# A routing-attention kernel: the first q and k loaded by tokens and turned by TensorE

## The chip, the core and the metric

The kernel runs on one core of a Trainium2 chip. Its engines are TensorE (matmuls, results into PSUM), VectorE, ScalarE and GpSimd (elementwise work), and SyncE, which issues DMAs; ScalarE issues some too. Each engine takes its instructions in order, and they meet by semaphores. The metric is the device time of one execution in microseconds (us): the median of several runs. Beside it stands one profiled execution, whose trace the views below are made from.

## The reference

An attention block with a mask by clusters, followed by a feed-forward block. Cut to what matters:

```python
# q, k, v: (4, 8, 768, 64); centroids: (8, 16, 64)
q_assign = argmax(einsum('bhsd,hcd->bhsc', normed(q), normed(centroids)))
k_assign = argmax(einsum('bhsd,hcd->bhsc', normed(k), normed(centroids)))
mask = q_assign[:, :, :, None] == k_assign[:, :, None, :]
scores = where(mask, q @ k.T / sqrt(64), -1e9)
attn = softmax(scores)
x = (attn @ v), heads side by side: (3072, 512)
h = x @ w_in                       # (512, 2048)
g = h * erf(softplus(h))
out = g @ w_out                    # (2048, 512)
```

All of it is float32. The centroid with the greatest similarity decides a token's cluster; a query sees only the keys of its own cluster.

## The kernel before

**Staging.** Heads are worked in pairs: 4 batches of 4 pairs make 16, and a pair's two heads lie in partitions 0 to 63 and 64 to 127. For each pair the kernel needs q and k with the head dimension in the partitions and the 768 tokens in the columns (tiles `qT` and `kT`, 128 x 768, float32). Period by period (`period(p, i)`, lines 1432 to 1536) it makes scores on TensorE, exponentials on ScalarE, sums on GpSimd and the product with v on TensorE, while parts of the coming pairs and of the weights are prepared on the side. Behind the attention stands the feed-forward block, which is nearly all TensorE.

**How q and k come in.** `load` (lines 225 to 246) fetches q in four DMAs: for each head `e` and each half `g` of its 64 dimensions, 32 partitions take the tokens of a block, and within them 24 runs of 32 float32 numbers:

```python
queues[e if nm == "q" else e * g].dma_start(
    out=t[e * D + g * Q : e * D + (g + 1) * Q],
    in_=src[b, h0 + e, :, g * Q : (g + 1) * Q].rearrange("(n t) d -> t n d", t=Q),
)
```

A block of 32 tokens by 32 dimensions then lies the wrong way round, and VectorE's transpose, which turns each 32 x 32 block, makes `qT` of `in_q` in one instruction; the same for k. For pair 0, `queues` is SyncE and ScalarE (q half and half, k with one DMA on ScalarE and three on SyncE); line 260 then sets both to SyncE, and pair 1 is loaded into the tile `x_more` by eight DMAs.

**The prologue** (lines 253 to 279, 349 to 389, 1543 to 1600) is written out by hand, and `InOrder` (lines 126 to 139) keeps each engine's instructions in program order. It runs like this:

- The centroids come in by a DMA of their own and are normed by VectorE and ScalarE (the tile `pr`, of which `cn` is a part). TensorE transposes `cn` with the identity (`te.transpose`, line 1546, into `pct`, a part of the bank `turned`), and two ScalarE copies put it into `ccT`. This is called the pct transpose below.
- `warm(n, bank, rhs)` (lines 1539 to 1541) issues n matmuls whose results nobody reads: 13 of 256 columns on the still empty tile `pick` at the start, 4 of 384 columns on zeros behind the pct transpose, 9 more before the masks, and 2 between the steps of the maxima.
- `qT` and `kT` of pair 0 are made (lines 1550 and 1556). ScalarE casts them to bfloat16 (`vectors`: `qv`, `kv`).
- `similarities(0)` (lines 404 to 415) multiplies `ccT` with both halves of `qT` and of `kT`: four 32-column groups, each in two passes, into `turned`. `choose(0)` (lines 417 to 441) is a chain on VectorE: transpose to `sims`, maximum, comparison (`hot`), transpose to `hotT`.
- In between, eight VectorE copies (lines 1562 to 1569) fill `pick`, a 0/1 matrix made of `first`, which GpSimd builds; `products(0)` makes the first q-by-k products into a PSUM tile `sc`.
- `masks(0, ...)` (lines 447 to 469) multiply `pick` with `hotT` and write `qm` and `km`. `maxima_step(0, i)` (lines 473 to 504), six of them, multiply `qv` by `kv` and `qm` by `km` on TensorE and take the maximum over the keys by VectorE (`nmx`); they use the PSUM tiles `wide` and `also` in turn.
- Then the first period starts.

`ps_s` is a pool of two PSUM tiles of 128 x 2 x 512 that `sc` and `also` come from by turns; `wide` is a third such tile of its own. `stage` holds one `in_q` and one `in_k`, so the loads of pair 2 (`load_qk(2)`) wait until pair 0's have been read.

Of the kernel before, what the change touches and what calls it, by code (L numbers as in the profile page):

```python
# [9 lines left out]
F32 = mybir.dt.float32  # L10
# [9 lines left out]
P = 128  # L20
B, H, S, D = 4, 8, 768, 64
C = 16
NJ = S // P
Q = 32
NB = S // Q
HW = S // 2
QW = HW // 2
TW = QW + 1
HJ = NJ // 2
# [113 lines left out]
def kernel(  # L143
# [13 lines left out]
    te, ve, ae, ge = (  # L157
        InOrder(tc, e, in_order) for e in (nc.tensor, nc.vector, nc.scalar, nc.gpsimd)
    )
# [8 lines left out]
    turned = [ps.tile([P, 512], F32, name=f"turned{i}") for i in range(2)]  # L168
# [12 lines left out]
    def passing(name, bufs, **kw):  # L181
        return attention.enter_context(tc.tile_pool(name=name, bufs=bufs, **kw))

    ps_s = passing("ps_s", 2, space=PSUM)
    wide = passing("ps_w", 1, space=PSUM).tile([P, 2, 512], F32, name="wide")

    const = passing("fixed", 1)
    stage = passing("stage", 1)
# [4 lines left out]
    ident = const.tile([P, P], F32, name="ident")  # L193
    identb = const.tile([P, P], BF16, name="identb")
    first = const.tile([P, P], BF16, name="first")
    pick = const.tile([P, 2, P], BF16, name="pick")
# [15 lines left out]
    rows = [{nm: const.tile([P, S], F32, name=f"{nm}T{i}") for nm in "qk"} for i in range(2)]  # L212
# [5 lines left out]
    pairs = {}  # L218
    sy = InOrder(tc, nc.sync, in_order)
    queues = [sy, ae]  # L220

    def heads(p):
        return p // HP, 2 * (p % HP)

    def load(p, nm, src, pl):
        if p >= NPAIR:
            return
        b, h0 = heads(p)
        if nm == "v":
            t = pl.tile([P, NJ, 2, D], F32, name="in_v")  # L230
            for e in range(2):
                queues[0].dma_start(out=t[:, :, e], in_=src[b, h0 + e].rearrange("(j p) d -> p j d", p=P))
        else:

            if pl is None:
                t = x_more.rearrange("p a k t -> p (a k t)")[:, (nm == "k") * S : (1 + (nm == "k")) * S]
                t = t.rearrange("p (n t) -> p n t", t=Q)
            else:
                t = pl.tile([P, NB, Q], F32, name="in_" + nm)
            for e in range(2):  # L240
                for g in range(D // Q):
# [4 lines that stand above are left out]
        pairs.setdefault(p, {})[nm] = t  # L246
# [7 lines left out]
    cen = setup[:, 0:D]  # L254
    sy.dma_start(out=cen, in_=centroids.rearrange("h c d -> (h c) d"))

    load(0, "q", q, stage)
    tc.keep_in_program_order(nc.scalar.preload_act_table_set("natural_log_exp_and_others"))
    load(0, "k", k, stage)
    queues[1] = sy  # L260
    load_qk(1)

# [6 lines left out]
    for base, pattern, sign, op, fill in (  # L269
# [5 lines left out]
            out=first, in_=first, compare_op=op, fill=fill, base=base, pattern=pattern,  # L275
# [141 lines left out]
    def choose(p, spare=None, aside=False):  # L417

        if p >= NPAIR:
            return  # L420
        st = pairs[p]
        n = HW // C
        sims = routep.tile([P, HW], F32, name="sims")
        ve.transpose(out=sims, in_=st.pop("psim"))
        yield
        sim = sims.rearrange("p (g c) -> p g c", c=C)
        mx = (wide[:, 0] if spare is None else spare)[:, 512 - n :]
        ve.reduce_max(out=mx, in_=sim, axis=AX.X)
        yield
        hot = routep.tile([P, HW], BF16, name="hot")  # L430
        ve.tensor_tensor(
            out=hot.rearrange("p (g c) -> p g c", c=C), in0=sim,
            in1=mx.unsqueeze(2).to_broadcast([P, n, C]), op=ALU.is_equal,
        )
        yield
        if aside:
            st["aside"] = routep.tile([P, HW], BF16, name="aside")
            ve.transpose(out=st["aside"][D + Q :], in_=hot[D : D + Q])
            yield
        st["hotT"] = routep.tile([P, HW], BF16, name="hotT")  # L440
        ve.transpose(out=st["hotT"], in_=hot)
# [84 lines left out]
    def products(u):  # L526
        p, half, j = units[u]
        if u in sc_of:
            return
        st = pairs[p]  # L530
        sc = sc_of[u] = ps_s.tile([P, 2, 512], F32, name="sc", tag="s")
        for e in range(2):
            r = slice(e * D, (e + 1) * D)
            te.matmul(
                sc[:, e, 0:HW], lhsT=st["kT"][r, j * P : (j + 1) * P],
                rhs=st["qT"][r, half * HW : (half + 1) * HW], start=True, stop=False,
            )
# [874 lines left out]
    def run(work):  # L1412
        for _ in work:
            pass
# [124 lines left out]
    def warm(n, bank, rhs):  # L1539
        for _ in range(n):  # L1540
            te.matmul(bank[:, 0 : rhs.shape[-1]], lhsT=identb, rhs=rhs, start=True, stop=True)

    zeros = lowest[1].rearrange("p t n -> p (t n)")
    warm(13, turned[1], pick.rearrange("p h n -> p (h n)"))
    pct = turned[0][:, 0:P]
    te.transpose(out=pct, in_=cn.rearrange("p e d -> p (e d)"), identity=ident)
    warm(4, turned[1], zeros)
    st = pairs[0]
    st["qT"], st["kT"] = rows[0]["q"], rows[0]["k"]
    ve.transpose(out=st["qT"], in_=st.pop("q").rearrange("p n t -> p (n t)"))  # L1550
    for e in range(2):
        ae.copy(
            out=ccT[e * D : (e + 1) * D, :, e * C : (e + 1) * C],
            in_=pct[e * D : (e + 1) * D].rearrange("d (r e c) -> d r e c", e=2, c=C)[:, :, e],
        )
    ve.transpose(out=st["kT"], in_=st.pop("k").rearrange("p n t -> p (n t)"))
    st.update(lows[0])
    load_qk(2)
    similarities(0)
# [2 lines left out]
    for r in (0, D):  # L1562
        for half in range(2):
            for e in range(2):
                c = r + half * Q + e * C
                ve.tensor_copy(
                    out=pick[r : r + D, half, e * D : (e + 1) * D].rearrange("p (n c) -> p n c", n=2)[:, :, 1 : C + 1],
                    in_=first[r : r + D, c : c + C].unsqueeze(1).to_broadcast([D, 2, C]),
                )
    also = ps_s.tile([P, 2, 512], F32, name="sc", tag="s")  # L1570
    products(0)
    warm(9, turned[0], zeros)
    run(choose(0))
    copies = [
        masks(0, nm, half, bank)
# [144 lines left out]
```

## Time and profile before

| What | Value |
|---|---|
| Median of 3 runs | 950.66 us (950.62 to 950.67) |
| Profiled execution, its own time | 950.97 us |
| Its span, first to last instruction | 949.2 us |
| DMA in all | 136.15 MB, 143 GB/s on average |
| TensorE's granted clock, all 40 slices | 0.9 or more |

How to read the views: a row of the page's groups names line, engine, operation, output and inputs, how often, busy time, mean time of one in ns, and the idle time before. Nearly all operations here have the line 134, that of the helper `InOrder`, so rows are told apart by their tiles. PE is TensorE, PEld its weight loads, DVE VectorE, ACT ScalarE, POOL GpSimd, SP SyncE; a "q" behind the name is the engine's queue, where DMAs are issued. In a timeline row the first number is the start in us, the second the stretch that the row covers, and the bracket behind tells how long the engine was idle before and what ended that. Matmul ends are modelled.

### The profile page before, as it was taken

The page shows a single profiled execution, that of the slowest core. Times are in us where ns is not written, and L with a number is a line of the kernel's source. Part 1 is how long each engine was busy: PE and PEld are TensorE (multiplying, and loading weights), DVE is VectorE, ACT ScalarE, POOL GpSimd, SP SyncE. Part 2 cuts the span into 40 slices and gives each one's busy share as a digit, 9 for nine tenths or more (in the row PEclk, how much of TensorE's full clock was granted, in tenths as well). Part 3 has the DMA queues.
Part 4 walks back from the last instruction along what each step waited for, and adds up shares of the span by engine and source line. Part 5 has one row for each costly group of instructions (what it writes and reads, how often), then busy time and mean ns, then how long its engine had stood idle before and what let it go on. Part 6 is the DMA issues. An engine that isn't in the chain of part 4 may idle for free.

```text
span 949.2 us, 20906 instructions
## 1 busy us (share of the span) xinstructions
PE 941.6 (99%) x8167; PEld 695.6 (73%) x8167; DVE 752.9 (79%) x1310; ACT 554.8 (58%) x852; POOL 557.5 (59%) x381
## 2 busy tenths in 40 slices
PE   8999999999999999999999999999999999999998
PEld 3555555555555555588888888888888888888887
DVE  8888888888888887788879878456786974768977
ACT  3788888888887665557523542357825225675341
POOL 1688888888888888845779930576600028770000
PEclk9999999999999999999999999999999999999999
DMA  9444544647454314292895486556645435533443
GB/s 208 93 114 107 116 108 109 156 113 200 91 113 107 71 34 146 81 326 67 164 192 212 155 238 216 156 155 175 191 141 182 156 112 154 171 97 114 153 133 111
DMA packets 181730, 136.15 MB, mean 143 GB/s; under 512 B 131808, under 2 KB 141536, under 8 KB 181600
## 3 DMA queue, kind: packets, MB, share of 16 engines
q1 hardware_dynamic: 174416, 125.21, 45.9%
q0 software_dynamic: 4720, 9.18, 5.5%
q8 instruction: 65, 1.06, 0.5%
q10 hardware_dynamic: 2496, 0.43, 0.2%
q14 instruction: 33, 0.27, 0.1%
HBM read 95.72 MB, written 40.89 MB: 144 GB/s over the span
## 4 chain that ended last, share of the span: by engine, by line
PE 97%; DVE 1%; DMA 0%; ACT 0%; issue 0%; DVEq 0%
PE bank L134 45%; PE turned L134 30%; PE sc L134 17%; PE wide L134 6%; DVE nmx L134 1%; DMA pr<-in_centroids_dram 0%; DMA in_q<-in_q_dram 0%; DVE pr L134 0%; ACT pr L134 0%; DVE sims L134 0%; DVE qT L134 0%; ACT qm L134 0%; DVE turned L134 0%; DVE wide L134 0%; ACT km L134 0%
## 5 line engine op out<-in xcount | busy, mean ns | idle before, releaser
L134 POOL TENSOR_TENSOR more_out<-more_out,pr 128x768 f32<-128x768 f32 x128 | 222.4, 1738 | 17.5 <-ACT pr L134 9.7
L134 DVE TENSOR_REDUCE nmx<-wide 128x2 f32<-128x512 f32 (+2 forms) x189 | 180.7, 956 | 57.8 <-PE wide L134 56.8
L134 ACT ACTIVATE pr<-sc 128x768 f32<-128x768 f32 x192 | 148.6, 810 | 71.5 <-PE wide L134 63.9
L134 PE MATMUL turned<-pr,in_v 128*32 128x193 f32 x3072 | 144.9, 330 | 0.0
L134 PEld LDWEIGHTS turned<-pr,in_v 128*32 128x32 f32 x3072 | 91.5, 109 | 51.5 <-issue 25.5
L134 PE MATMUL sc<-qT,kT 64*128 64x384 f32 x528 | 98.7, 487 | 0.0
L134 POOL TENSOR_TENSOR more_out<-pr,pr 128x768 f32<-128x768 f32 x32 | 58.7, 1834 | 46.6 <-ACT pr L134 46.6
L134 POOL TENSOR_TENSOR u<-w_in 128x1 f32<-128x1 f32 x2 | 0.4, 189 | 138.6 <-DVE w_in L134 138.6
L134 PE MATMUL bank<-x_own,more_in 128*128 128x256 f32 x280 | 69.1, 379 | 0.0
L134 PE MATMUL bank<-g_more,more_in 128*128 128x256 f32 x288 | 66.5, 380 | 0.0
L134 PE MATMUL wide<-kv,qv 64*128 64x256 bf16 (+2 forms) x378 | 64.2, 328 | 1.3 <-DVE nmx L134 0.7
L134 DVE TENSOR_TENSOR g<-g 128x512 f32<-128x512 f32 x70 | 48.6, 695 | 19.3 <-PE bank L134 12.3
L134 PE MATMUL wide<-km,qm 64*128 64x256 bf16 (+3 forms) x378 | 62.6, 327 | 0.0
L134 PEld LDWEIGHTS sc<-qT,kT 64*128 64x128 f32 x528 | 48.0, 187 | 19.5 <-ACT inv L134 3.2
L134 PEld LDWEIGHTS bank<-g_more,more_in 128*128 128x128 f32 x288 | 54.6, 190 | 8.2 <-DVE g L134 0.8
L134 PEld LDWEIGHTS bank<-x_own,more_in 128*128 128x128 f32 x280 | 53.2, 190 | 7.2
L134 DVE TENSOR_TENSOR g<-g,bank 128x256 f32<-128x256 f32 (+1 forms) x85 | 41.9, 511 | 20.4 <-PE bank L134 12.7
L134 ACT ACT_TABLE_LOAD x36 | 46.2, 1283 | 18.4 <-DVE g L134 17.8
L134 PE MATMUL bank<-w_out,g 128*128 128x256 f32 x240 | 55.2, 379 | 0.0
L134 DVE TENSOR_TENSOR g<-a_s,g 128x512 f32<-128x512 f32 x56 | 51.8, 941 | 2.7 <-ACT a_s L134 2.7
L134 PEld LDWEIGHTS <-qv 64*128 64x128 bf16 x384 | 22.8, 93 | 41.4 <-issue 25.3
L134 ACT ACTIVATE x_own<-x_own 128x512 int32<-128x512 uint32 (+2 forms) x52 | 52.7, 1028 | 0.0
(253 smaller groups left out, 2148.3 us busy)
## 6 DMA issues: line engine op xcount, KB each, us to landing
more_in<-a_dram SPq DMA_DIRECT2D x98, 256.0 KB, 2.7
g_more<-b_dram SPq DMA_DIRECT2D x48, 512.0 KB, 3.6
x_own<-in_moe_w_in_dram SPq DMA_DIRECT2D x13, 512.0 KB, 3.6
in_v<-in_v_dram SPq DMA_DIRECT2D x32, 192.0 KB, 3.1
x_dram<-more_out SPq DMA_DIRECT2D x128, 48.0 KB, 2.5
a_dram<-w_in SPq DMA_DIRECT2D x12, 512.0 KB, 5.0
x_own<-x_dram SPq DMA_DIRECT2D x6, 1024.0 KB, 5.9
in_k<-in_k_dram SPq DMA_DIRECT2D x59, 96.0 KB, 2.7
```

The lines of the kernel that those rows point to most:

```text
L134: ins = getattr(self.engine, name)(*args, **kw)
```

## The change

Four things. First, pair 0's q and k are no longer fetched by `load`, but with the tokens in the partitions: two DMAs each, one a head, one on SyncE and one on ScalarE, 768 runs of 64 numbers each. Second, TensorE turns them: six transposes with the identity for q into `wide`, six for k into a tile of `ps_s`; ScalarE copies the one to `qT`, VectorE the other to `kT`. These stand ahead of the pct transpose. VectorE's two block transposes go. Third, the eight copies into `pick` move from VectorE to GpSimd. Fourth, of the matmuls of `warm` there are 5 instead of 13, 3 instead of 4 and 8 instead of 9. The loading of the activation table on ScalarE now stands behind both of its DMAs, as before behind its two q loads.

Behind the prologue the two kernels have the same instructions in the same order on each engine.

```diff
-    load(0, "q", q, stage)
+    by_token = {}
+    for nm, src in (("q", q), ("k", k)):
+        t = stage.tile([P, NB, Q], F32, name="in_" + nm).rearrange("p n t -> p (n t)")
+        by_token[nm] = t.rearrange("p (j e d) -> p j e d", j=NJ, e=2)
+        for e in range(2):
+            queues[e].dma_start(out=by_token[nm][:, :, e], in_=src[0, e].rearrange("(j p) d -> p j d", p=P))
     tc.keep_in_program_order(nc.scalar.preload_act_table_set("natural_log_exp_and_others"))
-    load(0, "k", k, stage)
     queues[1] = sy
     load_qk(1)
...
     zeros = lowest[1].rearrange("p t n -> p (t n)")
-    warm(13, turned[1], pick.rearrange("p h n -> p (h n)"))
+    warm(5, turned[1], pick.rearrange("p h n -> p (h n)"))
+    st = pairs[0] = {}
+    rooms = {"q": wide, "k": ps_s.tile([P, 2, 512], F32, name="sc", tag="s")}
+    for nm in "qk":
+        for j in range(NJ):
+            te.transpose(
+                out=rooms[nm][:, j // HJ, j % HJ * P : (j % HJ + 1) * P],
+                in_=by_token[nm][:, j].rearrange("p e d -> p (e d)"), identity=ident,
+            )
+        st[nm + "T"] = rows[0][nm]
+        copy = ae.copy if nm == "q" else ve.tensor_copy
+        copy(out=st[nm + "T"].rearrange("p (h t) -> p h t", h=2), in_=rooms[nm][:, :, 0:HW])
     pct = turned[0][:, 0:P]
     te.transpose(out=pct, in_=cn.rearrange("p e d -> p (e d)"), identity=ident)
-    warm(4, turned[1], zeros)
-    st = pairs[0]
-    st["qT"], st["kT"] = rows[0]["q"], rows[0]["k"]
-    ve.transpose(out=st["qT"], in_=st.pop("q").rearrange("p n t -> p (n t)"))
+    warm(3, turned[1], zeros)
     for e in range(2):
         ae.copy(
             out=ccT[e * D : (e + 1) * D, :, e * C : (e + 1) * C],
             in_=pct[e * D : (e + 1) * D].rearrange("d (r e c) -> d r e c", e=2, c=C)[:, :, e],
         )
-    ve.transpose(out=st["kT"], in_=st.pop("k").rearrange("p n t -> p (n t)"))
     st.update(lows[0])
...
                 c = r + half * Q + e * C
-                ve.tensor_copy(
+                ge.tensor_copy(
...
     products(0)
-    warm(9, turned[0], zeros)
+    warm(8, turned[0], zeros)
     run(choose(0))
```

## The prediction

> **What bounds the kernel now.** I read the page first: engine shares, then the chain that ended last.
>
> ```profile
> span 949.2 us, 20906 instructions
> ...
> PE 941.6 (99%) x8167; PEld 695.6 (73%) x8167; DVE 752.9 (79%) x1310; ACT 554.8 (58%) x852; POOL 557.5 (59%) x381
> ...
> PE 97%; DVE 1%; DMA 0%; ACT 0%; issue 0%; DVEq 0%
> ...
> L134 ACT ACTIVATE pr<-sc 128x768 f32<-128x768 f32 x192 | 148.6, 810 | 71.5 <-PE wide L134 63.9
> ```
>
> TensorE is the chain for 97% of the span, so whatever the changed prologue gains or loses moves the rest one for one: the order of the instructions behind the prologue is the same in both kernels, and their loads can only be issued earlier. The prologue is the stretch in which TensorE is not the bound. So I read its timeline, engine by engine (start, length, engine, operation, what ended the idle time before it): SyncE's queue, TensorE, VectorE, ScalarE, GpSimd.
>
> ```profile
> 1.26 0.98 SPq L134 DMA_DIRECT2D in_q<-in_q_dram  x2
> 2.29 2.10 SPq L134 DMA_DIRECT2D in_k<-in_k_dram  x3
> ```
>
> ```profile
> 2.41 2.96 PE L134 MATMUL turned<-pick,identb 128*128 128x256 bf16 x13 [2.41 <-DVE fixed L134]
> 5.54 0.45 PE L134 MATMUL turned<-ident,pr 128*128 128x128 f32 x1 [0.17 <-DVE pr L134]
> 5.78 1.49 PE L134 MATMUL turned<-lowest,identb 128*128 128x384 bf16 x4
> 7.19 0.82 PE L134 MATMUL turned<-qT,ccT 128*32 128x384 f32 x2
> 7.70 0.57 PE L134 MATMUL turned<-kT,ccT 128*32 128x384 f32 x2
> 7.83 0.50 PE L134 MATMUL turned<-qT,ccT 128*32 128x384 f32 x2
> 8.10 0.49 PE L134 MATMUL turned<-kT,ccT 128*32 128x384 f32 x2
> 8.52 0.92 PE L134 MATMUL sc<-qT,kT 64*128 64x384 f32 x4
> 9.37 1.64 PE L134 MATMUL turned<-lowest,identb 128*128 128x384 bf16 x9
> 11.07 0.32 PE L134 MATMUL wide<-hotT,pick 64*128 64x384 bf16 x1
> ```
>
> ```profile
> 4.97 0.42 DVE L134 TENSOR_SCALAR pr<-pr 128x64 f32<-128x64 f32 x2
> 5.30 0.97 DVE L134 STREAM_TRANSPOSE qT<-in_q 128x768 f32<-128x768 f32 x1
> 6.66 0.98 DVE L134 STREAM_TRANSPOSE kT<-in_k 128x768 f32<-128x768 f32 x1 [0.39 <-DMA in_k<-in_k_dram]
> 7.57 0.80 DVE L134 COPY pick<-first 64x32 bf16<-64x32 bf16 x8
> 8.64 0.58 DVE L134 STREAM_TRANSPOSE sims<-turned 128x384 f32<-128x384 f32 x1 [0.28 <-PE turned L134]
> 9.26 0.56 DVE L134 TENSOR_REDUCE wide<-sims 128x24 f32<-128x384 f32 x1
> 9.85 0.55 DVE L134 TENSOR_TENSOR hot<-sims,wide 128x384 bf16<-128x384 f32 x1
> 10.44 0.58 DVE L134 STREAM_TRANSPOSE hotT<-hot 128x384 bf16<-128x384 bf16 x1
> 11.43 0.56 DVE L134 TENSOR_SCALAR qm<-wide 128x384 bf16<-128x384 f32 x1 [0.41 <-PE turned L134]
> 11.90 0.97 DVE L134 STREAM_TRANSPOSE qT<-x_more 128x768 f32<-128x768 f32 x1
> 12.79 0.92 DVE L134 TENSOR_REDUCE nmx<-wide 128x2 f32<-128x768 f32 x1
> ```
>
> ```profile
> 6.02 0.42 ACT L134 COPY ccT<-turned 64x64 f32<-64x64 f32 x2 [1.92 <-PE turned L134]
> ```
>
> ```profile
> 2.87 0.77 POOL L134 MEMSET lowest<- 128x384 bf16 x2
> ```
>
> What to see: the last k load lands at 6.66 (VectorE was waiting for it), kT ends at 7.64, the k similarities follow at 7.70 and end at 8.59, then `sims` to `hotT` on VectorE until 11.02, the mask matmuls at 11.07, and VectorE's chain of maxima from 12.79. So one number decides: the end of the k similarities, 8.59 us. The eight pick copies lie behind kT, but VectorE still waits 0.28 us for TensorE after them: they cost nothing now.
>
> TensorE's own rate changes here too. In the row of 4 a 384-column matmul takes some 0.32 us from start to start, in the row of 9 (1.64 less 0.33 for the last, by 8) 0.16. The first q pair takes 0.64 to its second pass (7.19 to 7.83), the k pair's second pass only 0.40 (7.70 to 8.10): full rate comes at about 7.8, 5.4 us after the first matmul. The profile's granted clock reads 1.00 throughout and doesn't show it.
>
> **The loads.** Removed are eight loads of 96 KB (four of q, four of k) in runs of 32 numbers, 128 bytes; added are four of 192 KB in runs of 64, 256 bytes: half the packets, the same 786 kB. The centroids (33 kB) stay ahead. Rates, from the view of stretches (last columns: DMA share, GB/s), and a load's time to landing, from the view of DMA issues:
>
> ```profile
> 1.50:2.00 0.50, 0.00 (x0) 0.00 (x0) 0.26 (x6) 0.17 (x1) 0.43 (x7) 1.00 0.15 33
> 2.00:2.50 0.50, 0.09 (x1) 0.10 (x2) 0.41 (x7) 0.50 (x1) 0.43 (x2) 1.00 1.09 184
> 3.50:4.00 0.50, 0.50 (x4) 0.38 (x3) 0.13 (x1) 0.30 (x2) 0.14 (x1) 1.00 1.37 213
> 5.00:5.50 0.50, 0.36 (x2) 0.00 (x0) 0.50 (x3) 0.00 (x0) 0.00 (x0) 1.00 1.39 216
> 5.50:6.00 0.50, 0.46 (x2) 0.36 (x3) 0.50 (x1) 0.00 (x0) 0.00 (x0) 1.00 0.97 150
> 48.25:48.50 0.25, 0.25 (x4) 0.00 (x0) 0.25 (x1) 0.25 (x1) 0.25 (x1) 1.00 1.08 244
> ```
>
> ```profile
> in_q<-in_q_dram SPq DMA_DIRECT2D x1, 96.0 KB, 3.2
> ```
>
> The first row puts the first bytes near 1.95 us; the next three are the rate with 128-byte runs while loads are queued; the row at 48 us is a stretch in which only in_v moves, whose loads have the very form of the new ones. The last is q's last load (issued near 1.72): landed near 4.9. I take 244 GB/s. The bounds: 216 (longer runs bring nothing) and 314 (244 if packets overlapped on the engines as at 5 us, 1.39 over 1.08). From last byte to landing I take 0.4 us (an estimate: at 184, some 213 and then 150 GB/s the 819 kB of centroids, q and k end near 6.0, and k lands at 6.66, so 0.6; the faster bound is 0.3).
>
> k: 819 kB by 244 is 3.36 us after 1.95, and 0.4: landed at 5.7 (bounds 4.9 and 6.3). q: SyncE's half starts moving near 2.45 (issued at 1.26, with the 1.15 us of the first load) and shares the engines with ScalarE's queue: 197 kB at 122 is 1.6 us, and 0.4: landed at 4.45 (4.0 to 4.85). So q comes 0.5 and k 1.0 us earlier.
>
> [...]
>
> SyncE's queue reaches the eight x_more loads some 2 us sooner, behind its k load; the second in_q and in_k loads now wait for TensorE's transposes instead of VectorE's, and are issued earlier than today in any case. Nothing behind them in that queue (in_v, weights) is read in these 13 us.
>
> **The transposes.** Removed from VectorE: 0.97 + 0.98 us and 0.80 us of copies. Added on TensorE: 12 transposes of the form of the pct row, which is 0.24 us from its start (5.54) to the next matmul's (5.78) and 0.45 us to its end; then a 768-column copy out of PSUM on ScalarE (0.81, the exp row) and one on VectorE (0.92, the nmx row). At half rate, bounds per transpose: 0.11 (half of the 0.23 of a 256-column warm matmul) and 0.29 (its weights, loaded each time, not hidden); I take 0.24, its own row. All 12 lie before 7.8, so at half rate:
>
> - the 5 warm matmuls end at about 3.6; TensorE waits for q until 4.50; everything behind it in its queue waits too, but of it only the pct transpose (its data ready at 5.39) would have had something to do before 6 us.
> - q's six: 4.50 to 5.94; ScalarE's copy 6.2 to 7.0, hidden behind what follows.
> - k's six: k is there at 5.7, so 5.94 to 7.38; the last starts at 7.14 and ends at 7.59.
> - kT copy on VectorE: 7.62 to 8.54 (now 7.64).
> - pct goes behind the k transposes: 7.38 to 7.83, ccT's two copies to 8.28 (now 6.44): hidden behind kT by 0.26 us.
> - k similarities from 8.60 (0.06 after kT, as now): 0.89 us now (7.70 to 8.59), 0.08 less at full rate, where the passes lie 0.32 apart instead of 0.40: end 9.41.
>
> 9.41 against 8.59 is 0.82 us later. What the loads gain, the longer way from landing to kT (six transposes behind q's six, then a copy of 0.92, against one transpose of 0.98) gives back and more.
>
> **What costs nothing.** Eight warm matmuls fewer, and one each of 4 and 9: TensorE waits for others there; eight after the products (1.3 us) end before `hotT`, 2.4 us after the similarities. The pick copies on GpSimd start at 3.6 (behind its memsets and the warm matmuls that read pick); at the 0.39 us of its memset row each they end by 6.8, at VectorE's 0.1 by 4.4; the masks need them after 11. Without that cover the masks would wait. VectorE's copy now waits on TensorE, with `sims` behind it, which needs it anyway.
>
> **Sum.** +0.8 us. The profiled execution took 950.97 us, 949.2 in the span and 1.8 around it; the median is 950.66, which I start from: 951.5. This case's own range, with loads and transposes some way towards their bounds: 950.9 to 952.2.
>
> **Rivals.**
> 1. *The clock comes late* (slower). TensorE's dense run is broken at 3.6. If the wait and the transposes don't count as work, the 5.4 us begin with the three warm matmuls at 7.6, and full rate comes at 13.0: similarities to 10.1 (two half-rate passes), products 1.3, eight warm matmuls at 0.32 until 13.0, so the masks start near 13.4 instead of 11.07: +2.3, 953.0; if the release falls half way, near 10.5, +1.4. It decides once products and warm matmuls (2.2 us at full rate) take longer than VectorE's 2.4. For it: the five warm matmuls left. Against: from 4.5 on TensorE has work without a break, as from 2.4 now. No row shows a run of transposes, so I leave it a fifth. [...]
> 2. *The loads win* (not slower). With 314 GB/s and 0.16 us a transpose: q at 4.0, k's six from 5.0 to 6.2, kT at 7.15 against 7.64, similarities 0.5 earlier: 950.2. For it: the share of 1.39 reached with two queues. Against: in_v stays at 244 with two loads queued.
> 3. *It doesn't do what it says to the end*: gains and losses meet within 0.2 us because k lands when the transposes are through: 950.7.
>
> **Numbers.** Forecast 0.45, clock late 0.18, loads win 0.27, even 0.10. Faster or slower by 0.2% means 1.9 us, about what a measurement of this kernel can tell from no change. Even with everything favourable kT cannot be ready before 6.4 (k at 4.9, six at 0.11, copy), a gain of some 1.1, so faster is 0.03; slower is half of the late clock, 0.09; within 0.88. Range: 949.9 (most of the second rival) to 953.0 (most of the first).
>
> **What would show it.** In the changed profile: k's landing near 5.7, q's transposes starting near 4.5 at 0.24 us apart, kT's copy ending near 8.5, `sims` starting near 9.5 instead of 8.64, masks near 11.9, the first maximum near 13.6. I am wrong if k's transposes start before 5.2 or are closer than 0.18 (second rival), or if the matmuls behind pct are 0.32 us apart after 8 us (first); wrong altogether if rows behind 20 us shift by another amount than `sims` does.

## The result, and the profile after

| | Before | Changed |
|---|---|---|
| Median, us | 950.73 (950.61 to 951.18, 18 runs) | 952.66 (952.12 to 953.46, 18 runs) |
| Ratio | | 1.0020, interval 1.0013 to 1.0028 |
| Profiled execution, own time / span | 950.97 / 949.2 | 952.28 / 950.6 |
| Highest less lowest run | 0.57 | 1.34 |

The changed kernel is 1.9 us slower. Of that, 1.4 is in the span of its profiled execution; the rest isn't in that one, and the runs scatter more than twice as far as before.

The page's span, its engine shares and the chain that ended last, of the changed kernel:

```profile
span 950.6 us, 20904 instructions
...
PE 941.8 (99%) x8169; PEld 696.3 (73%) x8169; DVE 751.3 (79%) x1301; ACT 555.3 (58%) x853; POOL 558.5 (59%) x389
...
PE 97%; DVE 1%; SPq 1%; DMA 0%; ACT 0%; issue 0%; DVEq 0%
```

TensorE is 97% of the chain as before. New is SyncE's queue with 1%, but it bounds nothing. The chain in order of time steps from VectorE's transpose of `x_more` at 12.86 back to the landing, at 12.44, of a load of pair 2's q, and from there along the queue's issues from 9.33 to 0.82. The transpose doesn't read that load: pair 1's q, which it does read, had landed by 7.75, and it starts as VectorE ends `qm`. (The page infers releasers from semaphore events.) What TensorE does wait for at the start, q's landing, is in its timeline of the prologue (start, length, operation, idle time before and what ended it):

```profile
2.41 1.25 PE L134 MATMUL turned<-pick,identb 128*128 128x256 bf16 x5 [2.41 <-DVE fixed L134]
4.61 1.51 PE L134 MATMUL wide<-ident,in_q 128*128 128x128 f32 x6 [0.95 <-DMA in_q<-in_q_dram]
5.92 1.50 PE L134 MATMUL sc<-ident,in_k 128*128 128x128 f32 x6
7.21 0.42 PE L134 MATMUL turned<-ident,pr 128*128 128x128 f32 x1
7.43 1.17 PE L134 MATMUL turned<-lowest,identb 128*128 128x384 bf16 x3
8.53 0.59 PE L134 MATMUL turned<-qT,ccT 128*32 128x384 f32 x2
8.54 0.58 PE L134 MATMUL turned<-kT,ccT 128*32 128x384 f32 x2
8.94 0.49 PE L134 MATMUL turned<-qT,ccT 128*32 128x384 f32 x2
8.95 0.49 PE L134 MATMUL turned<-kT,ccT 128*32 128x384 f32 x2
12.03 0.32 PE L134 MATMUL wide<-hotT,pick 64*128 64x384 bf16 x1 [0.33 <-DVE hotT L134]
```

And of VectorE:

```profile
7.46 0.96 DVE L134 COPY kT<-sc 128x768 f32<-128x768 f32 x1 [1.97 <-PE sc L134]
9.52 0.58 DVE L134 STREAM_TRANSPOSE sims<-turned 128x384 f32<-128x384 f32 x1 [1.10 <-PE turned L134]
11.39 0.58 DVE L134 STREAM_TRANSPOSE hotT<-hot 128x384 bf16<-128x384 bf16 x1
13.75 0.92 DVE L134 TENSOR_REDUCE nmx<-wide 128x2 f32<-128x768 f32 x1
```

k's six transposes take 1.50 less the last one's 0.42, by 5: 0.21 us each, against 0.24 of the pct row before. kT is ready at 8.42 (7.64 before), all similarities run from 8.53 to 9.44 (the k ones ended at 8.59), `sims` starts 0.88 later than before, the masks (12.03 against 11.07) and the first maximum (13.75 against 12.79) 0.96 later. (The additional 0.07 arises right behind `sims`: in every kernel made from the changed one the row after it starts 0.69 after it, in the others 0.62.) The three matmuls behind pct start 0.32 apart, the two passes of the similarities some 0.41: full rate came near 8.7, not at 7.8.

Behind the prologue the shift of the rows of TensorE and VectorE stays at 0.95 to 0.96 until 107 us. There it grows to 1.18, and at the very end by another 0.24, which makes the 1.4 of the span.

### The profile page after: what moved, and what is told of

It reads as the page before. It is cut to its first block, busy times and chain, and to the rows that moved or that the text cites. A ratio compares the mean times of both kernels' runs of the same rounds, so it can differ in the third digit from the quotient of the medians.

```text
span 950.6 us, 20904 instructions
## 1 busy us (share of the span) xinstructions
PE 941.8 (99%) x8169; PEld 696.3 (73%) x8169; DVE 751.3 (79%) x1301; ACT 555.3 (58%) x853; POOL 558.5 (59%) x389
## 3 DMA queue, kind: packets, MB, share of 16 engines
q8 instruction: 65, 1.06, 0.5%
## 4 chain that ended last, share of the span: by engine, by line
PE 97%; DVE 1%; SPq 1%; DMA 0%; ACT 0%; issue 0%; DVEq 0%
PE bank L134 45%; PE turned L134 30%; PE sc L134 17%; PE wide L134 6%; SPq L134 1%; DVE nmx L134 1%; DMA in_q<-in_q_dram 0%; DVE qT L134 0%; ACT qm L134 0%; ACT pr L134 0%; DVE sims L134 0%; DVE turned L134 0%; ACT km L134 0%; DVE osb L134 0%; DVE lowest L134 0%
```

## The experiments

Each is a small edit of one of the two kernels. Ratios are to runs of the kernel before on the same chip, whose medians lay between 950.73 and 950.80. `sims` is where the first transpose to it starts in the profiled execution; "tail" is the time there from the last landing of a DMA to the end of the span. Each experiment has 11 runs, number 12 has 5. An interval is some 0.9 us to either side (1.3 for number 12), so what is said below of tenths rests on the traces of the profiled executions, one a kernel, and not on the medians.

| Experiment | Based on | Median (lowest to highest) | Ratio to before, interval | `sims` | Tail |
|---|---|---|---|---|---|
| before | | 950.73 | | 8.64 | 0.97 |
| changed | | 952.66 (952.12 to 953.46) | 1.0020 (1.0013 to 1.0028) | 9.52 | 1.21 |
| 1 ten warm matmuls | changed | 952.28 (951.55 to 952.81) | 1.0016 (1.0007 to 1.0025) | 9.40 | 1.21 |
| 2 five warm matmuls | before | 951.91 (951.28 to 952.61) | 1.0012 (1.0004 to 1.0021) | 9.23 | 0.97 |
| 3 pick on GpSimd | before | 950.72 (950.55 to 951.03) | 1.0000 (0.9991 to 1.0009) | 8.41 | 0.97 |
| 4 four DMAs more | before | 951.05 (950.91 to 951.29) | 1.0003 (0.9994 to 1.0012) | 8.55 | 1.21 |
| 5 q by tokens only | changed | 950.96 (950.82 to 951.57) | 1.0002 (0.9993 to 1.0011) | 8.33 | 1.10 |
| 6 the same, early start | changed | 951.02 (950.87 to 951.13) | 1.0002 (0.9993 to 1.0011) | 8.30 | 1.09 |
| 7 early start | changed | 951.76 (951.47 to 952.09) | 1.0010 (1.0001 to 1.0019) | 9.04 | 1.21 |
| 8 early start | before | 950.78 (950.54 to 950.90) | 0.9998 (0.9990 to 1.0007) | 8.48 | 0.97 |
| 9 two DMAs more | before | 951.05 (950.97 to 951.26) | 1.0003 (0.9994 to 1.0012) | 8.60 | 1.34 |
| 10 number 5, four DMAs more | changed | 951.24 (950.95 to 951.61) | 1.0005 (0.9996 to 1.0014) | 8.72 | 1.34 |
| 11 four DMAs more | changed | 952.40 (951.88 to 952.89) | 1.0016 (1.0007 to 1.0025) | 9.94 | 0.97 |
| 12 VectorE's stream longer | changed | 954.44 (953.81 to 954.87) | 1.0038 (1.0024 to 1.0052) | 10.83 | 1.22 |

### 1. The five missing warm matmuls put back

```diff
-    warm(5, turned[1], pick.rearrange("p h n -> p (h n)"))
+    warm(10, turned[1], pick.rearrange("p h n -> p (h n)"))
```

> The changed kernel with 10 warm matmuls at the start instead of 5, so that TensorE works without a break from 2.4 us until q has landed (10 x 0.213 us after 2.41 is 4.55; q lands at 4.48 in the changed kernel's profile). Theory A (the clock: full rate comes some time after TensorE's dense work began, at a point that differs between executions; the break from 3.66 to 4.61 sets that beginning 2.2 us later): the profiled execution keeps its sums (first similarities after 8.0, first maximum within 0.3 of 13.75), the median falls by 0.4 to 0.9, to 951.8 to 952.3, and the spread of the runs from 1.3 (952.12 to 953.46) to 0.7 or less. Rival B (the spread comes from when the loads land): median 952.5 to 952.8, spread still above 1. Rival C (only the longer path of k counts, the spread is chance): median within 0.15 of 952.66.

The median fell by 0.38, just short of the 0.4 that was expected; the spread stayed at 1.26, which is what rival B had. In the trace the pause before q's transposes is gone (the ten end at 4.72, the transposes start at 4.57) and full rate comes near 8.0. That the pause mattered is likely, but 0.38 is little beside either kernel's spread and isn't clear of it. Closing the pause doesn't bring the steadiness of the kernel before. That the path to kT now runs on TensorE and on its rate would explain it. Rival B, the landing of the loads, isn't excluded as a part; but number 7 below has the same loads and a spread of 0.62, so the loads alone don't make 1.26.

### 2. Only the warm matmuls taken from the kernel before

```diff
-    warm(13, turned[1], pick.rearrange("p h n -> p (h n)"))
+    warm(5, turned[1], pick.rearrange("p h n -> p (h n)"))
```

> The kernel before with one edit: 5 warm matmuls at the start instead of 13; loads, transposes and copies as before. TensorE then rests from 3.6 to 5.5 us. Theory A (the clock): full rate comes later than 7.8 us, in most executions between 9 and 12; similarities and warm matmuls run at half rate for longer, the masks start 0.4 to 1.2 us later than 11.07, the median is 951.2 to 951.9 and the runs spread over more than 0.9 us (0.57 before). Rival C (nobody waits for these matmuls, so they are worth nothing): 950.6 to 950.9, spread as before.

Everything else is as before: blocks loaded, VectorE's transposes. It costs 1.2 us of the median all the same, and the spread widens to 1.33. TensorE's timeline of this kernel:

```profile
2.41 1.25 PE L134 MATMUL turned<-pick,identb 128*128 128x256 bf16 x5 [2.41 <-DVE fixed L134]
5.44 0.45 PE L134 MATMUL turned<-ident,pr 128*128 128x128 f32 x1 [1.78 <-DVE pr L134]
7.74 0.85 PE L134 MATMUL turned<-qT,ccT 128*32 128x384 f32 x2
8.33 0.85 PE L134 MATMUL turned<-kT,ccT 128*32 128x384 f32 x2
9.11 1.48 PE L134 MATMUL sc<-qT,kT 64*128 64x384 f32 x4
10.52 1.64 PE L134 MATMUL turned<-lowest,identb 128*128 128x384 bf16 x9
12.09 0.33 PE L134 MATMUL wide<-hotT,pick 64*128 64x384 bf16 x1
```

The second passes take 0.85 where before they took 0.50 and 0.49, the four products 1.48 where they took 0.92: TensorE is still at half rate at 9 us. The k loads landed at the same time (6.63 against 6.64), so nothing but TensorE's rate can have moved the masks to 12.09, past those of the changed kernel. VectorE's rows tell how:

```profile
9.23 0.58 DVE L134 STREAM_TRANSPOSE sims<-turned 128x384 f32<-128x384 f32 x1 [0.88 <-PE turned L134]
11.03 0.58 DVE L134 STREAM_TRANSPOSE hotT<-hot 128x384 bf16<-128x384 bf16 x1
```

`sims` starts 0.59 later than before. `hotT` is ready at 11.61, but the masks stand behind the nine warm matmuls, which the slow products have pushed to 10.52: that is the other 0.43 of the 1.02. So matmuls whose results nobody reads were on the path here, first by being absent and then by standing in the way. "Full rate at 7.8" was no fixed time of this program; it was bought with the thirteen matmuls. Nor did it come at a fixed time after the first matmul: 5.4 us after it in the kernel before, 3.2 in number 8 below, whose first matmuls start 0.21 us apart up to 4.30 and 0.11 from there. That the moment also differs between executions of one kernel is theory A's estimate and not shown, with one profiled execution a kernel. The spreads agree with it in part: 0.57 with early dense work, 1.33 and 1.34 without, but 1.26 in number 1 with it.

### 3. Only the pick copies moved to GpSimd

```diff
-                ve.tensor_copy(
+                ge.tensor_copy(
```

> The kernel before with one edit: the eight copies into pick on GpSimd instead of VectorE. Prediction's reading (VectorE waited 0.28 us for TensorE behind them anyway): the start of sims stays within 0.05 of 8.64 and the median within 0.1 of the kernel before. Rival (the copies were on the path, or disturb VectorE's short chain before 5.4 us from GpSimd): sims moves by more than 0.1 one way or the other.

The ratio is 1.0000, and the copies, now on GpSimd, are over long before the masks need them:

```profile
3.81 1.38 POOL L134 COPY pick<-first 64x32 bf16<-64x32 bf16 x8 [0.18 <-POOL lowest L134]
```

But `sims` started at 8.41, 0.23 early, where at most 0.05 was expected and the rival asked for 0.1. In that execution k landed at 6.47 instead of 6.64, which is 0.17 of it; TensorE's full rate came earlier as well (q's similarities took 0.97 us from first start to last end, 1.14 before). Whether the copies have a hand in that, one profiled execution doesn't tell; the median shows neither a gain nor a price.

### 4, 9 and 11. How many DMAs there are in all

The changed kernel has four DMAs fewer than the one before. Its last landing is 1.21 us ahead of the end of the span, before it was 0.97. In these three, pair 0's v comes in by more DMAs, two a head for number 9 and three for numbers 4 and 11, and nothing else changes:

```diff
-                queues[0].dma_start(out=t[:, :, e], in_=src[b, h0 + e].rearrange("(j p) d -> p j d", p=P))
+                for js in ((0, 2), (2, 4), (4, 6)) if p == 0 else ((0, NJ),):
+                    js = slice(*js)
+                    queues[0].dma_start(
+                        out=t[:, js, e], in_=src[b, h0 + e].rearrange("(j p) d -> p j d", p=P)[:, js]
+                    )
```

> The kernel before with pair 0's v loaded by six DMAs instead of two, the same bytes: four DMAs more in all, where the change has four fewer, so that the last output DMA of the program signals by the same one of eight semaphores in turn as in the changed kernel. Theory D (SyncE's last waits, done in a fixed order, are 0.2 us longer then): from the landing of the last output DMA to the end of the span 1.2 us instead of 0.97, the median 0.15 to 0.3 above the kernel before. Rival (that tail is chance): 0.97, median within 0.1.

> The kernel before, with pair 0's v fetched by four DMAs instead of two (two more on SyncE's queue in all). Theory 'last semaphores' (the end of the program has SyncE pass over the DMAs' semaphores in a fixed order, about 0.06 us each, and only those behind the one that lands last cost anything): with two DMAs more none stands behind it, so last landing to end of span falls from 0.97 to about 0.85 us, and the median is 0.1 us below that of the kernel before. Rival 'each DMA costs': the tail grows or stays at 0.97 or above.

> The changed kernel with pair 0's v fetched by six DMAs instead of two, so that it has as many DMAs as the one before. Theory 'last semaphores': tail back from 1.21 to 0.97 us, prologue as in the changed kernel (sims at 9.5), median 0.2 below it: 952.3 to 952.5. Rival 'the tail is the prologue's doing': tail stays at 1.2.

| DMAs in all | kernels | tail, us |
|---|---|---|
| 546 | changed, 1, 7, 12 | 1.21 to 1.22 |
| 548 | 5, 6 | 1.10, 1.09 |
| 550 | before, 2, 3, 8, 11 | 0.97 |
| 552 | 9, 10 | 1.34 |
| 554 | 4 | 1.21 |

Number 4 gives the kernel before the tail of the changed one, number 11 takes it from the changed one, so the tail is the count's doing and not the prologue's. Number 11's prologue wasn't that of the changed kernel, as had been expected (`sims` at 9.94 instead of 9.5): q landed at 4.90 there and not at 4.48. Number 9 missed its figure and told the rest: two more don't bring 0.85 but 1.34. The tail falls by 0.12 for two DMAs and starts again behind 550; 546 and 554 are alike, which is one turn of a cycle of eight. SyncE's records in the traces show what stands behind it. The last nine DMAs signal eight semaphores by turns, and at the end SyncE waits for the eight in a fixed order; those already signalled pass 0.06 us apart. In the kernel before, the last DMA signals the seventh and one wait is left behind it; in the changed kernel it is the third (five left). Counted on by turns from these two, it is the fifth in number 5 (three left), the third in number 4 (five left) and the first in number 9 (seven left). The tail is 0.91 us and 0.06 for each wait that is left. In the view of DMA issues and the timeline the tail can be read from the last load: in the kernel before the last output DMA was issued at 946.48 and landed 1.7 us later, 0.97 before the end at 949.18.

```profile
946.48 0.37 ACTq L1365 DMA_DIRECT2D out_dram<-osb  x1
```

In the changed kernel it was issued at 947.64 and landed at 949.37, but the span ends at 950.58:

```profile
947.64 0.36 ACTq L1369 DMA_DIRECT2D out_dram<-osb  x1
```

### 5, 6 and 10. Each of q and k by the way that suits it

q keeps the new way, since it has time until k is there. k goes back to blocks and VectorE's transpose, as this spares it the queue behind q on TensorE. Number 6 adds the early start of number 7 below to number 5, number 10 the split of v of number 4.

```diff
-    for nm, src in (("q", q), ("k", k)):
+    for nm, src in (("q", q),):
...
     tc.keep_in_program_order(nc.scalar.preload_act_table_set("natural_log_exp_and_others"))
+    load(0, "k", k, stage)
...
-    warm(5, turned[1], pick.rearrange("p h n -> p (h n)"))
+    warm(10, turned[1], pick.rearrange("p h n -> p (h n)"))
...
+            if j == 4:
+                te.transpose(out=pct, in_=cn.rearrange("p e d -> p (e d)"), identity=ident)
...
+    ae.copy(out=st["qT"].rearrange("p (h t) -> p h t", h=2), in_=wide[:, :, 0:HW])
+    st["kT"] = rows[0]["k"]
+    ve.transpose(out=st["kT"], in_=st.pop("k").rearrange("p n t -> p (n t)"))
```

> Half of the change: q alone by tokens and through TensorE (its copy to qT on ScalarE, the pct transpose between q's fourth and fifth, ccT's copies ahead of qT's), k by blocks and turned by VectorE as before; 10 warm matmuls so that TensorE has no break before q lands; pick on GpSimd. Theory A with the path of k (the loss is six more transposes and a copy between k's landing and kT; loads by tokens do help): k lands near 6.1 instead of 6.64, kT near 7.1, the k similarities end near 8.1 instead of 8.59, median 950.2 to 950.6, spread below 0.8. Rival B (loads by tokens land late or at changing times): median 950.9 or more.

> The mixed kernel with the first 15 warm matmuls using pick as weights too, which VectorE clears first, so that TensorE starts at about 1.1 us instead of 2.4. Theory A: full rate comes 1.3 us earlier on average, q's transposes and the similarities run at full rate more often; median 0.1 to 0.3 below the mixed kernel, spread below 0.6. Rival C (the clock plays no part here): within 0.1 of the mixed kernel.

> The mixed prologue (q by tokens through TensorE, k by blocks through VectorE), with pair 0's v fetched by six DMAs instead of two, so that the whole kernel has two DMAs more than the one before. Theory 'last semaphores': tail about 0.85 us instead of 1.10, so 0.25 us below the mixed kernel: 950.6 to 950.8, sims at 8.3 as in it. If 'each DMA costs': tail above 1.10.

The prologue does gain, as this view of VectorE in number 5 shows:

```profile
6.32 0.98 DVE L134 STREAM_TRANSPOSE kT<-in_k 128x768 f32<-128x768 f32 x1 [0.86 <-DMA in_k<-in_k_dram]
8.33 0.58 DVE L134 STREAM_TRANSPOSE sims<-turned 128x384 f32<-128x384 f32 x1 [1.03 <-PE turned L134]
...
12.55 0.92 DVE L134 TENSOR_REDUCE nmx<-wide 128x2 f32<-128x768 f32 x1
```

kT starts 0.34 and the first maximum 0.24 us sooner than before. But the kernel doesn't: 0.12 of it goes into the tail (548 DMAs), 0.2 into a stall near 180 us of the kind that number 12 is about. So the median is 950.96, where rival B had it, and not 950.2 to 950.6, though not for the rival's reason: k landed at 6.19. Number 6 was to gain another 0.1 to 0.3; it gained 0.03 in `sims` and nothing in the median, as rival C had it, only the spread fell to 0.26. Number 10 was to take the tail away and took the worst place of the cycle (552), with the stall as well. Its prologue is number 5's, but `sims` started at 8.72: the second passes of the similarities start 0.64 us after the first, 0.34 in number 5, so full rate came later in that execution. None of the three is faster than the kernel before.

### 7 and 8. Full rate before the transposes begin

```diff
-    def warm(n, bank, rhs):
+    def warm(n, bank, rhs, lhsT=identb):
...
-    warm(5, turned[1], pick.rearrange("p h n -> p (h n)"))
+    warm(15, turned[1], pick.rearrange("p h n -> p (h n)"), pick[:, 0])
```

The zeros of `pick` serve as weights too, and `pick` is cleared first, so that TensorE starts at 1.13 instead of 2.41. Number 8 does the same to the kernel before, with 19.

> The changed kernel with the first warm matmuls (15 instead of 5) using pick as weights too, cleared first: TensorE works from 1.1 us and without a break until q lands. Theory A: as the 12 transposes, the similarities and the warm matmuls behind them all run on TensorE, their time falls with the clock's release 1.3 us earlier than in the kernel with 10 warm matmuls (952.28) and 3.5 us earlier than in the changed kernel (952.66): median 951.5 to 951.9, no run above 952.5. Floor by the path alone, with everything at full rate: 12 transposes save up to 1.3 us. Rival C: within 0.15 of 952.28.

> The kernel before with the same early start of TensorE (19 warm matmuls from 1.1 us, so that they end near 5.2 as now). Theory A: its path waits for loads and VectorE, and only the k similarities (0.1 us) and the last warm matmuls gain: median 950.5 to 950.75, spread no larger than before. Rival C: 950.73 to within 0.05.

Number 7 came as expected: the changed kernel gets 0.9 us faster, and each of its 11 runs is below each of the changed kernel's 18. Number 8's median of 950.78 lies just above the 950.5 to 950.75 of theory A and within rival C's 0.05; either way the early start is worth next to nothing there. TensorE in number 7:

```profile
1.13 3.20 PE L134 MATMUL turned<-pick 128*128 128x256 bf16 x15 [1.13 <-DVE pick L134]
4.99 0.84 PE L134 MATMUL wide<-ident,in_q 128*128 128x128 f32 x6 [0.65 <-DMA in_q<-in_q_dram]
6.26 0.84 PE L134 MATMUL sc<-ident,in_k 128*128 128x128 f32 x6 [0.42 <-DMA in_k<-in_k_dram]
```

and VectorE behind it:

```profile
7.14 0.96 DVE L134 COPY kT<-sc 128x768 f32<-128x768 f32 x1 [1.76 <-PE sc L134]
9.04 0.58 DVE L134 STREAM_TRANSPOSE sims<-turned 128x384 f32<-128x384 f32 x1 [0.94 <-PE turned L134]
```

Six transposes take 0.84 instead of 1.5, about 0.11 each (0.84 less the last one's 0.27, by 5). Even so `sims` starts 0.4 us later than before: k landed at 6.12 there, and from landing to kT it is 1.98 us (six transposes and a copy out of PSUM) where VectorE's one transpose took 1.00 from a landing at 6.64. Here the way through TensorE is priced with all of it at full rate.

The transposes of row 6.26 ran at full rate: 0.11 us each, about half of the 0.21 of the same row in the changed kernel. Whether transposes alone can bring full rate, the runs don't settle, since plain matmuls lie before and behind them in all. But in the changed kernel full rate came near 8.7, 1.3 us after the first plain matmul behind them (7.43). In number 2, which has the same five matmuls at the start and no such transposes, it came between 9.9 and 10.5 (the products are at half rate, the nine matmuls behind them at full rate), at least 4.4 us after the pct transpose (5.44). So the twelve seem to have counted.

### 12. A longer instruction stream on VectorE

In the changed kernel and in numbers 1, 7 and 11, VectorE starts the `sims` near 107 us 0.13 us after it is free, where in the kernel before it starts 0.09 us ahead of the end of the instruction before it. TensorE's next matmuls into `turned` wait for that (at 108.44; they belong to the seventh `divide`, the step that sums a block's exponentials and divides by them). Rows of VectorE before:

```profile
105.40 1.23 DVE L134 TENSOR_REDUCE nmx<-wide 128x2 f32<-128x1024 f32 x1 [0.56 <-PE wide L134]
106.54 0.57 DVE L134 STREAM_TRANSPOSE sims<-turned 128x384 f32<-128x384 f32 x1
```

and in the changed kernel, 1.35 instead of 1.14 from start to start:

```profile
106.35 1.23 DVE L134 TENSOR_REDUCE nmx<-wide 128x2 f32<-128x1024 f32 x1 [0.56 <-PE wide L134]
107.70 0.58 DVE L134 STREAM_TRANSPOSE sims<-turned 128x384 f32<-128x384 f32 x1
```

Neither kernel has an instruction between. The last semaphore event of VectorE lies 0.24 us ahead of `sims` before and 0.45 in the changed kernel, so it isn't what ended the wait. What differs is where VectorE is in its stream: its stream is nine instructions shorter by then (thirteen with its semaphore waits). And an 8 KB packet of an instruction queue moves just behind the stall (108.4). So:

```diff
+    spare = const.tile([P, 8], F32, name="spare")
+    for i in range(8):
+        ve.memset(spare[:, i : i + 1], 0.0)
     warm(5, turned[1], pick.rearrange("p h n -> p (h n)"))
```

> The changed kernel with eight tiny memsets more on VectorE, in the time in which it waits for k's transposes: nothing is computed otherwise, but VectorE's instruction stream is eight longer ahead of everything else (the change had made it nine shorter). Theory 'instruction load': the 0.13 us by which VectorE starts the seventh `sims` transpose late (near 107.7 us, with an 8 KB packet of an instruction queue at 108.4) is a fetch of its next 128 instructions, and it moves about four us ahead, to a place where VectorE is waiting anyhow; then the seventh divide starts 0.14 after the instruction before it, the shift against the kernel before stays what `sims` (of pair 0) has, 0.2 us less than in the changed kernel, with the 8 KB packet near 104 instead of 108.4; the median is some 0.2 lower, which the spread of 1.3 us may hide. Rival 'the shifted schedule': the stall comes from where the other engines stand and stays at the seventh divide.

The stall at this place is gone, 1.14 from start to start:

```profile
107.67 1.23 DVE L134 TENSOR_REDUCE nmx<-wide 128x2 f32<-128x1024 f32 x1 [0.55 <-PE wide L134]
108.81 0.57 DVE L134 STREAM_TRANSPOSE sims<-turned 128x384 f32<-128x384 f32 x1
```

The 8 KB packet is at 101.5 instead of 108.4 (near 104 was expected). The shift against the changed kernel falls by 0.2 there, as the theory of the instruction load had it, and the rival, by which the stall stays, is out. But the stall wasn't put into a free moment; another came near 180 us, with another such packet at 179.8:

```profile
178.34 0.98 DVE L134 STREAM_TRANSPOSE more_out<-in_k 128x768 f32<-128x768 f32 x1 [0.35 <-issue]
179.24 0.65 DVE L134 TENSOR_REDUCE nmx<-wide 128x2 f32<-128x512 f32 x1
179.82 1.96 DVE L134 TENSOR_TENSOR w_in<-w_in,fixed 128x512 f32<-128x512 f32 x1
```

For 0.35 us ahead of the first row VectorE waited for nothing that is shown. The last row takes 0.68 in the changed kernel; what makes it 1.28 longer here isn't shown. Over these rows the shift against the changed kernel grows from 1.1 to 2.1 us.

The late start in numbers 5, 6 and 10 lies here too. In number 5 it is 1.33 from start to start:

```profile
178.20 1.23 DVE L134 TENSOR_REDUCE nmx<-wide 128x2 f32<-128x1024 f32 x1 [0.56 <-PE wide L134]
179.53 0.58 DVE L134 STREAM_TRANSPOSE sims<-turned 128x384 f32<-128x384 f32 x1
```

The places speak for the theory. Counted in the traces with its semaphore waits, the late instruction is the 192nd of VectorE's stream in the changed kernel and in 1, 7 and 11. It is the 320th in 5, 6 and 10, and in number 12, where a wait in front of the first row is late. The two places are 128 instructions apart, as many as the expectation gave an 8 KB packet (an estimate from the changed kernel's page agrees: 1.06 and 0.27 MB in the instruction queues for 20904 instructions are some 64 bytes for one, so 8 KB are some 128). But the place alone doesn't decide: the 320th isn't late in the changed kernel, nor the 192nd in number 5, and in the kernels made from the one before no row of VectorE up to 300 us is late against it by 0.1 us, but for the masks' wait in number 2. That the lateness is the loading itself is still argued.

The median of number 12 was to fall by 0.2 and rose by 1.8. About 1 us of its profile's loss lies in the rows near 180 us; the larger part, 1.3 us, is in the prologue, where the token loads were slow: 225 GB/s where the changed kernel had 278. The view of stretches of number 12 (last columns: DMA share, GB/s):

```profile
4.50:5.00 0.50, 0.00 (x0) 0.00 (x0) 0.43 (x3) 0.00 (x0) 0.50 (x4) 1.00 1.38 225
```

and of the changed kernel:

```profile
4.50:5.00 0.50, 0.39 (x2) 0.42 (x3) 0.43 (x3) 0.00 (x0) 0.50 (x4) 1.00 1.29 278
```

Why the same four loads moved more slowly there is open; the edit also adds a tile to on-chip memory, and a run with only the tile wasn't tried.

## Why the prediction was right, and where it wasn't

The sign and the place were right, and 952.66 lies in the range. The forecast of 951.5 is 1.2 us too low. The median also lies outside the 950.9 to 952.2 of the forecast's own case: what holds it is the end that the first rival gave the range, so that it was held isn't to the forecast mechanism's credit. And the 1.9 us are just the 0.2% at which the prediction set slower (0.09) apart from within (0.88). By its own steps:

- **The loads.** k at 5.7, q at 4.45: the changed kernel's profile has 5.77 and 4.48, although the queues moved 287 GB/s at 4 us and not 244; the start was slower (163 GB/s from 2.0 to 2.5 us), and by the packets in the trace SyncE's queue had moved k's last bytes near 5.07, 0.7 us before k landed and not 0.4. Two misses cancel there, which is luck. What was missed is that this is the fast end. In the five profiled kernels that load both by tokens, k landed at 5.77, 5.82, 6.12, 6.27 and 6.83; in the six that load blocks, between 6.47 and 6.66. The new loads are sooner, but less certain.
- **Transposes, copies, similarities.** k's transposes near 5.94, kT at 8.54, end at 9.41: measured 5.92, 8.42 and 9.44. The similarities of q didn't go ahead of k's: the third matmul behind pct, started at 8.07, stood before both, and all began at 8.53, 0.11 after kT. The sum of +0.8 for `sims` was +0.88; the masks came 0.13 later than the 11.9 that was said.
- **Eight warm matmuls fewer at no cost.** This step failed. It counted what TensorE would otherwise do in that time and took full rate at 7.8 for given. Number 2 prices the eight alone at 1.2 us in the kernel before. In the changed kernel full rate before the transposes is worth 0.9 (number 7), and a part of that, the half-rate transposes, was in the +0.8; five of the eight put back gained 0.38, not clear of the spread (number 1). Number 8 shows the other side: before, an earlier start buys nothing, since k's landing was the bound there (VectorE waits 0.47 us for it in number 8).
- **The first rival** ("the clock comes late") had that mechanism, and its two ends, 952.1 and 953.0, hold the median. Its test, matmuls behind pct 0.32 us apart after 8 us, came out, if only just: the third starts at 8.07. Number 2 shows the rest of it, products and warm matmuls that hold up the masks. But its reason was off: the transposes seem to have counted as work (full rate came 1.3 us after the first plain matmul behind them; without them, in number 2, at least 4.4 us after the pct transpose), and in the profiled execution full rate came 0.9 us late (near 8.7), not 5. It is the first rival in part. The profiled execution took 952.28, less than the median; what the slower ones spent, no trace shows.
- **The second rival** fell: k's transposes start at 5.92 and are 0.21 apart. The third too: the gains and losses didn't meet.
- **Pick copies on GpSimd at no cost:** number 3's median shows no price, and they end at 5.19 there.
- **"Wrong altogether if rows behind 20 us shift by another amount than `sims`"**: they do, by 0.07 from the row behind `sims`, by another 0.2 from 107 us on, and the end by another 0.24. The prologue's reading stands, but the sum lacked two terms that no view of the prologue shows: the number of DMAs in all (0.24, numbers 4 and 11) and the place at which VectorE stalls (0.2, number 12).

With number 7 the 1.9 us come apart like this: its first maximum is 0.48 later than before with TensorE at full rate (the longer way from k's landing), the stall 0.2, the tail 0.24, which is 0.9 against 1.0 of its median; and the 0.9 between it and the changed kernel is TensorE's rate, with the scatter of the loads in it. So the largest single term is TensorE's rate, of which the sum had only the half-rate transposes. The matmuls that were put at nothing set that rate in number 2; how much of the 0.9 is theirs in the changed kernel, no run separates.

## What to carry to other kernels

A matmul that computes nothing can still have a price (1.2 us for eight of them in number 2): before one is taken away, ask what TensorE's rate will be in the next microseconds, and try the removal alone. Moving work to TensorE early in a kernel made the path depend on that rate here (six transposes took 1.50 us at half rate, 0.84 at full), where VectorE's one transpose took 0.97 to 0.98 (before, and numbers 2 to 6 and 8 to 10). And when a change is worth a microsecond or less, compare the last row and a few far behind the change too, for the count of DMAs and the place in an engine's stream moved the time by tenths here (0.24 and 0.2 us) without touching what was edited.

## What the runs showed of the hardware

- The tail behind the last landing goes with the number of DMAs: 1.34, 1.21, 1.10 and 0.97 us for 552, 546 or 554, 548 and 550. SyncE's last waits are for eight semaphores in a fixed order, 0.06 us for each that is already signalled.
- TensorE's full rate came 5.4 us after the first matmul in the kernel before and 3.2 in number 8; without eight early matmuls (number 2) the masks came 1.02 us later and the median rose by 1.2.
- A float32 transpose of 128 x 128 on TensorE takes 0.21 us back to back at half rate and 0.11 at full rate.
- Eight memsets on VectorE, 0.17 us in all and far off the path, moved a late start from 107 to 178 us. In eight kernels such a start falls on the 192nd or the 320th instruction of its stream, 128 apart.
- Loads in runs of 256 bytes reached 287 GB/s from two queues where runs of 128 bytes reached some 216, and their landing varied by 1.1 us from kernel to kernel against 0.2.
